# Where SyncE waits for the output: inside the block, or behind its closing barrier

## The chip, the cores and the metric

The kernel runs on one core of one Trainium2 chip. A core has five engines with a queue of instructions each: TensorE (PE in the profile, with PEld for its weight loads), VectorE (DVE), ScalarE (ACT), GpSimd (POOL) and SyncE (SP). [...] Transfers are issued by SyncE and ScalarE and run on 16 DMA engines; when one lands, its semaphore has been raised by 16 in all.

The metric is the device time of one execution in microseconds (us). The time of the kernel before is the median of three runs.

## What is computed

One decode step of a transformer layer for two sequences, B = 2, with one new token each, D = 640. In short:

```python
W = min(4096, max(256, Sk // 4))                  # 2048 of the 8192 cached keys
q = layernorm(x) @ wq                             # 32 heads of 192
p = softmax(q . k_cache[:, :, -W:] * 192 ** -0.5)
h = x + (p . v_cache[:, :, -W:]) @ wo
h2 = h + (gelu(layernorm(h) @ w_gate) * (layernorm(h) @ w_up)) @ w_down
```

All inputs are bfloat16. Only the last 2048 positions of the two caches are read, but every head has its own keys and values, so 122 MB come from memory for an output of 2 x 640 numbers (2.5 KB).

## The kernel before

The kernel records every operation first and emits it afterwards. `_Prog` keeps a list of operations per engine, works out from the tiles that each reads and writes which semaphores it must wait for (`resolve`), and `emit` writes one engine's list in the order of recording. `emit_loop` does the same for TensorE, with a loop over four groups of heads.

Loads are all issued by SyncE (line 347) into one ring of SBUF with six slots: 16 loads of keys and 16 of values, 3072 KB each, the weights of the attention, and at the end those of the feed-forward part, `w_down` in four pieces last. A load waits on SyncE until the slot that it takes has been read. Keys are transposed by TensorE (line 555) and copied out by ScalarE and VectorE (lines 564 and 567); scores, softmax and the weighted values follow a group behind.

The end of the program is what matters here. The last matmuls take the four pieces of `w_down` (line 850), VectorE copies the result to the tile `yrow` (line 856), and ScalarE issues the store of the output (line 857), whose semaphore is called `dout`. Nothing reads the output on the chip.

The emitted lists stand in a block (from line 867). A block gives each engine its own stretch of code, and ends in a barrier of all five engines, which is written when the block is closed. In that barrier ScalarE, TensorE, VectorE and SyncE each drain their pipeline, raise a common semaphore by one and wait for a release; GpSimd waits until the four have come, and releases them. In the kernel before, the block is closed together with the other contexts, when the function ends; the profile puts the barrier's instructions down to line 241. In SyncE's list one wait is written by hand behind the loads, for `dout` to reach 16. In the built program that wait is carried by SyncE's branch to the end of the block, so it stands ahead of SyncE's part of the barrier.

Of the kernel before, what the change touches and what calls it, by code (L numbers as in the profile page):

```python
# [227 lines left out]
def bass_sequential_preLN__sliding_block_cached__geglu_ffn__decode_kernel(  # L228
# [12 lines left out]
    with ExitStack() as ctx:  # L241
# [84 lines left out]
        P = _Prog()  # L326
# [535 lines left out]
        sems = {}  # L862
        for e, c in (("pe", 0), ("act", 0), ("dve", 0), ("dve", 1), ("pool", 0)):
            sems[e, c] = ctx.enter_context(nc.semaphore(f"s_{e}{c}"))
        for d in P.dma_count:
            sems["d", d] = ctx.enter_context(nc.semaphore(f"s_{d}"))
        block = ctx.enter_context(nc.Block())

        @block.gpsimd
        def _(e):  # L870
            P.emit("pool", e, sems)

        @block.sync
        def _(e):
            P.emit("sp", e, sems)
            e.wait_ge(sems["d", "dout"], 16)

        @block.vector
        def _(e):
            P.emit("dve", e, sems)  # L880

        @block.scalar
        def _(e):
            P.emit("act", e, sems)

        @block.tensor
        def _(e):
            P.emit_loop(e, sems, 4, ["a0", (0, None, ["oc"]), "a1", (0, 3, ["op"]), "a2", "b0", "b1", "b2", "c0", "c1", "c2",
                                     (None, 3, ["d0", "d1", "d2"])])


# [26 lines left out]
```

## Time and profile before

| what | value |
|---|---|
| median of three runs | 294.08 us (293.97, 294.08, 294.17) |
| span of the profiled execution, first to last instruction | 292.4 us |
| around the span (median less span) | 1.7 us |
| TensorE matmul, busy | 196.2 us, 67% |
| VectorE, busy | 128.2 us, 44% |
| ScalarE, busy | 96.3 us, 33% |
| read from memory | 122.29 MB, 418 GB/s over the span |
| issue of the output's store | starts at 290.26 us, takes 0.64 us |
| last end of the barrier's instructions | 292.4 us |

The profile is of one execution; times in its views count from the first instruction of the span. The profile gives that execution's span and no device time of its own, so the 1.7 us is the difference between the profiled execution's span and the median of other executions. "Busy" leaves out waits, branches, semaphore instructions and the issuing of transfers, which the sequencer of an engine does; in views, these have a q behind the engine's name (SPq, ACTq). A page of a profile gives the chain of waits that ended last, the groups of instructions with their idle time, and the transfers; finer views list the waits of one engine, the instructions of one line of the source, and the instructions in order of time. The trace behind them also holds every change of a semaphore, with its time, and every packet of a transfer.

### The profile page before, as it was taken

How to read it: one execution, taken by the hardware profiler on the slowest of the kernel's cores; microseconds unless marked ns; L12 is line 12 of the kernel's file. 1: busy time of each engine (PE TensorE's matmuls, PEld its weight loads, DVE VectorE, ACT ScalarE, POOL GpSimd, SP SyncE). 2: the span in 40 equal slices, each digit the busy share in tenths (PEclk: the TensorE clock that was granted, in tenths of full speed). 3: DMA queues.
4: the chain of work that ended last, by engine and by line, in shares of the span. 5: the costliest groups of instructions: out<-in, count | busy, mean ns of one | idle time of the engine just before them, and what ended most of it. 6: DMA issues, size and time to landing. Idle time of an engine off the chain costs nothing.

```text
span 292.4 us, 5066 instructions
## 1 busy us (share of the span) xinstructions
PE 196.2 (67%) x2141; PEld 151.6 (52%) x2141; DVE 128.2 (44%) x311; ACT 96.3 (33%) x120; POOL 8.6 (3%) x36
## 2 busy tenths in 40 slices
PE   2450769848677298849493597659596959585584
PEld 1440436728475285628281575456566657563242
DVE  5950075713447045525264155425265535352231
ACT  2150116623442143616161154325342525341000
POOL 4000020000000000000000000000000000000000
PEclk9996679995979579998899599969797968897755
DMA  7997999999999999999999999999999999999993
GB/s 269 430 531 338 433 447 436 430 433 430 423 408 448 430 434 428 430 430 430 430 402 450 434 430 430 430 430 434 430 430 430 430 430 434 430 430 405 425 416 148
DMA packets 6362, 122.44 MB, mean 419 GB/s; under 512 B 718, under 2 KB 848, under 8 KB 1360
## 3 DMA queue, kind: packets, MB, share of 16 engines
q1 hardware_dynamic: 6336, 122.29, 97.9%
q8 instruction: 7, 0.11, 0.2%
q14 instruction: 3, 0.02, 0.0%
q10 hardware_dynamic: 16, 0.01, 0.0%
HBM read 122.29 MB, written 0.00 MB: 418 GB/s over the span
## 4 chain that ended last, share of the span: by engine, by line
DMA 76%; PE 20%; SPq 2%; DVE 1%; issue 0%
DMA ring<-in_A_k_cache_dram 57%; PE tps L555 15%; DMA ring<-in_A_wq_dram 10%; DMA ring<-in_B_w_down_dram 10%; PE tps L576 2%; SPq L347 2%; PE ops L657 1%; PE m L708 1%; PE m L690 1%; DVE ktr L567 0%; DVE ering L408 0%; PE m L850 0%; PE m L641 0%; PE m L671 0%; DVE yrow L856 0%
## 5 line engine op out<-in xcount | busy, mean ns | idle before, releaser
L555 PE MATMUL tps<-identf,ring 128*128 128x128 f32 x768 | 114.4, 317 | 45.4 <-DMA ring<-in_A_k_cache_dram 44.1
L555 PEld LDWEIGHTS tps<-identf,ring 128*128 128x128 f32 x768 | 105.5, 166 | 48.4 <-DMA ring<-in_A_k_cache_dram 45.4
L564 ACT ACTIVATE ktr<-tps 128x1024 bf16<-128x1024 bf16 x80 | 79.4, 1023 | 84.0 <-PE tps L555 84.0
L567 DVE COPY ktr<-tps 128x1024 bf16<-128x1024 bf16 x112 | 74.0, 687 | 71.3 <-PE tps L555 70.4
L632 ACT ACTIVATE eexp<-sm,nm 128x512 bf16<-128x512 f32 x16 | 11.5, 721 | 64.1 <-DVE nm L630 64.1
L657 PE MATMUL ops<-ring,ering 128*32 128x384 bf16 x512 | 24.7, 337 | 4.8 <-DMA ring<-in_A_v_cache_dram 4.7
L613 PE MATMUL sps<-ktr,rq 128*16 128x512 bf16 x384 | 25.8, 403 | 1.1 <-POOL rq L408 1.1
L621 DVE CUSTOM_DVE_ANT_1 sm<-sps,mska 128x512 f32<-128x512 f32 x16 | 11.1, 692 | 34.9 <-PE sps L613 34.9
L657 PEld LDWEIGHTS ops<-ring,ering 128*32 128x32 bf16 x512 | 12.7, 98 | 13.3 <-DMA ring<-in_A_v_cache_dram 6.2
L613 PEld LDWEIGHTS sps<-ktr,rq 128*16 128x16 bf16 x384 | 9.5, 90 | 11.9 <-issue 2.1
L628 PEld LDWEIGHTS m<-mrhs,pm 128*128 128x128 bf16 x16 | 1.5, 96 | 22.8 <-DVE mrhs L404 22.8
L576 PE MATMUL tps<-ring,xnT 128*32 128x384 bf16 x80 | 5.7, 472 | 10.9 <-DMA ring<-in_A_wq_dram 10.9
L628 PE MATMUL m<-mrhs,pm 128*128 128x16 bf16 x16 | 2.9, 183 | 14.7 <-DVE mrhs L404 14.7
L408 POOL TENSOR_TENSOR rq<-qs,mask 128x96 bf16<-128x96 bf16 x16 | 5.6, 359 | 195.4 <-PE sps L613 161.3
L576 PEld LDWEIGHTS tps<-ring,xnT 128*32 128x32 bf16 x80 | 3.1, 134 | 13.4 <-issue 11.1
L599 DVE CAST qs<-ops 128x384 bf16<-128x384 f32 x1 | 0.6, 558 | 17.7 <-PE ops L594 17.7
L408 DVE TENSOR_TENSOR ering<-m,mask 128x256 bf16<-128x256 f32 x16 | 6.7, 419 | 3.2 <-PE m L641 3.2
L708 PE MATMUL m<-ring,ot 128*2 128x320 bf16 x96 | 4.7, 340 | 2.4 <-DMA ring<-in_A_wo_dram 2.4
L583 ACT ACTIVATE qrow<-tps 128x768 bf16<-128x768 f32 x1 | 0.8, 812 | 15.6 <-PE tps L576 15.6
L788 ACT ACTIVATE lnv<-tps,eps_t 98x1 f32<-98x1 f32 x1 | 0.3, 262 | 17.3 <-PE tps L786 17.3
L641 PE MATMUL m<-sel,eexp 128*128 128x64 bf16 x64 | 5.0, 206 | 1.2 <-ACT eexp L632 1.2
L641 PEld LDWEIGHTS m<-sel,eexp 128*128 128x128 bf16 x64 | 4.7, 111 | 1.7 <-DVE nm L630 1.3
(124 smaller groups left out, 88.8 us busy)
## 6 DMA issues: line engine op xcount, KB each, us to landing
ring<-in_A_k_cache_dram SPq DMA_DIRECT2D x16, 3072.0 KB, 31.2
ring<-in_A_v_cache_dram SPq DMA_DIRECT2D x16, 3072.0 KB, 27.3
ring<-in_A_wq_dram SPq DMA_DIRECT2D x1, 7680.0 KB, 28.3
ring<-in_A_wo_dram SPq DMA_DIRECT2D x4, 1920.0 KB, 21.5
ring<-in_B_w_gate_dram SPq DMA_DIRECT2D x1, 1920.0 KB, 31.5
ring<-in_B_w_up_dram SPq DMA_DIRECT2D x1, 1536.0 KB, 24.8
ring<-in_B_w_down_dram SPq DMA_DIRECT2D x1, 960.0 KB, 27.2
ring<-in_B_w_down_dram SPq DMA_DIRECT2D x1, 480.0 KB, 27.9
```

What stands on the lines that cost most here:

```text
L347: P.op("sp", lambda e, v=v, src=src: e.dma_start(v, src), W=toks + [("sem", sem)], dma=sem)
L408: return lambda e: e.tensor_tensor(out=out, in0=a, in1=b, op=op)
L555: ins = e.transpose(tps[bi][:, 128 * u:128 * (u + 1)], kv[:, off:off + 128], identf[:, :])
L564: act(lambda e, dst=dst, bv=bv: e.activation(out=dst, in_=bv, func=ACT.Copy), W=[("kt", n)], X=[("t", bi)])
L567: dve(lambda e, dst=dst, bv=bv: e.tensor_copy(dst, bv), W=[("kt", n)], X=[("t", bi)], cls=0)
L576: ins = e.matmul(tps[0][32 * r:32 * (r + 1), 0:384], lhsT=xnT[:, c, 32 * J:32 * (J + 1)], rhs=wq[:, c, 1536 * J + 384 * r:1536 * J + 384 * ...
L613: ins = e.matmul(sps[32 * ch:32 * ch + 16, :], lhsT=rq[:, g % 4, k, :], rhs=ktr[:, k // 2, 1024 * ch + k % 2:1024 * (ch + 1):2], start=(k ...
L621: dve(lambda e: e.tensor_tensor_reduce(out=sm[:, :].rearrange("p (u x) -> p u x", u=4), in0=sps[:, :].rearrange("p (u x) -> p u x", u=4), ...
L632: act(lambda e: e.activation(out=eexp[:, :], in_=sm[:, :], func=ACT.Exp, bias=nm[:, 0:1], scale=1.0, accum_out=zr[:, g % 4:g % 4 + 1]), R= ...
L641: ins = e.matmul(o, lhsT=eexp[:, 128 * u:128 * (u + 1)], rhs=sel64[:, :], start=True, stop=True)
L657: ins = e.matmul(ops_[32 * r:32 * (r + 1), 0:384], lhsT=ering[:, g % 4, t, :], rhs=vv[:, 384 * t:384 * (t + 1)], start=(g % 4 == 0 and t < 4),
L708: ins = e.matmul(m1[32 * r:32 * r + 2, 192:512], lhsT=ot[:, kk, :], rhs=wo[:, kk - k0, 320 * h:320 * (h + 1)], start=(kk == 1 or J < 2 and ...
```

## The change

The block is closed by a `with` statement of its own, and SyncE's wait for `dout` is written behind it, outside the block. So SyncE's branch to the end of the block waits for nothing, the barrier of the five engines is built as before (the profile will have it under line 867), and one more instruction stands behind it on SyncE alone: a wait until `dout` is 16 (line 890). The order and the waits of all other instructions of the five engines are the same. Only the indentation of the rest of the block changes.

```diff
-        block = ctx.enter_context(nc.Block())
+        with nc.Block() as block:
...
-        @block.sync
-        def _(e):
-            P.emit("sp", e, sems)
-            e.wait_ge(sems["d", "dout"], 16)
+            @block.sync
+            def _(e):
+                P.emit("sp", e, sems)
...
+        nc.sync.wait_ge(sems["d", "dout"], 16)
```

More of the change, by code (lines that the diff above doesn't have):

```diff
@@ L866, in bass_sequential_preLN__sliding_block_cached__geglu_ffn__decode_kernel, with _ @@
             sems["d", d] = ctx.enter_context(nc.semaphore(f"s_{d}"))
-        block = ctx.enter_context(nc.Block())
-        @block.gpsimd
-        def _(e):
-            P.emit("pool", e, sems)
-        @block.sync
-        def _(e):
-            P.emit("sp", e, sems)
-            e.wait_ge(sems["d", "dout"], 16)
[L878 to L889, printed above, removed]
+        with nc.Block() as block:
+            @block.gpsimd
+            def _(e):
+                P.emit("pool", e, sems)
+            @block.sync
+            def _(e):
+                P.emit("sp", e, sems)
+            @block.vector
+            def _(e):
+                P.emit("dve", e, sems)
+            @block.scalar
+            def _(e):
+                P.emit("act", e, sems)
+            @block.tensor
+            def _(e):
+                P.emit_loop(e, sems, 4, ["a0", (0, None, ["oc"]), "a1", (0, 3, ["op"]), "a2", "b0", "b1", "b2", "c0", "c1", "c2",
+                                         (None, 3, ["d0", "d1", "d2"])])
+        nc.sync.wait_ge(sems["d", "dout"], 16)
 _INS = ['A_x', 'A_k_cache', 'A_v_cache', 'A_wq', 'A_wo', 'B_x', 'B_w_gate', 'B_w_up', 'B_w_down']
```

## The prediction

> **What bounds the kernel now**
>
> I read the page first, for the share of each engine and of the transfers; then the chain of waits to its last step; then the waits of SyncE's queue, since the edit moves one of them; then the instructions of the line on which the closing barrier is put down (L241). The page:
>
> ```profile
> span 292.4 us, 5066 instructions
> ...
> HBM read 122.29 MB, written 0.00 MB: 418 GB/s over the span
> ...
> DMA 76%; PE 20%; SPq 2%; DVE 1%; issue 0%
> ```
>
> The kernel is bound by reading 122 MB; its chain is 76% transfers. Nothing there is touched. The end of the chain:
>
> ```profile
> 260.85 28.24 DMA ring<-in_B_w_down_dram
> 289.09 0.04 issue
> 289.14 0.74 PE m L850 x12
> 289.88 0.02 issue
> 289.91 0.32 DVE yrow L856
> ```
>
> The last weights land at 289.09, twelve matmuls and one copy follow, and the chain of working instructions stops at 290.23. The span has 2.1 us more. The timeline's only line behind that copy, and SyncE's longest late wait:
>
> ```profile
> 290.26 0.64 ACTq L857 DMA_DIRECT2D out_dram<-yrow  x1
> ```
>
> ```profile
> SPq L241 <- DMA out_dram<-yrow: 26.4, 1, 26.4
> ```
>
> SyncE issued its last load by 265.6 and then sat 26.4 us on the output's semaphore. Nothing but the closing barrier stands behind that wait on its queue, but four other engines stand in the barrier. The barrier's own instructions (count, duration in ns min/median/max, first and last start):
>
> ```profile
> engine op xcount: duration ns min/median/max, first and last start us, forms
> L241 POOLq EVENT_SEMAPHORE  x2: 17/17/17, 292.2 to 292.3; - x2
> L241 POOLq DRAIN  x1: 457/457/457, 204.2 to 204.2; - x1
> L241 PEldq DRAIN  x1: 372/372/372, 289.5 to 289.5; - x1
> L241 DVEq DRAIN  x1: 364/364/364, 289.9 to 289.9; - x1
> L241 ACTq DRAIN  x1: 485/485/485, 290.9 to 290.9; - x1
> L241 SPq COMPARE_BRANCH  x1: 33/33/33, 292.0 to 292.0; - x1
> L241 SPq DRAIN  x1: 13/13/13, 292.2 to 292.2; - x1
> L241 SPq EVENT_SEMAPHORE  x1: 17/17/17, 292.3 to 292.3; - x1
> ...
> L241 PEldq EVENT_SEMAPHORE  x1: 51/51/51, 292.3 to 292.3; - x1
> ```
>
> The reader is to see the order: POOL, PE, DVE and ACT are drained long before SyncE. The trace's records have the same in ns, with the semaphore events, which no view prints. ACT's drain starts at 290.948 and its arrival is counted at 291.441. The output's last increment comes at 291.977; SyncE's branch, which carries the wait, runs at 291.994, its drain at 292.154, its arrival is counted at 292.168. POOL sees all four at 292.192 and releases them at 292.295; SyncE's last instruction ends at 292.329, PE's at 292.375, and that is the span's end.
>
> **What lies around the span.** The median of 294.08 is 1.7 us over the span. The records go on behind the span: semaphore 2, which the kernel does not own, is counted up five times at 292.614, .649, .859, .904 and .928, four times more at 293.029, .068, .104 and .151; then each engine clears a block of semaphores until 293.715, and the nine counts come again from 293.939 to 294.299. The same nine stand ahead of the kernel, from -0.372 to 0.001. There the engines start their first instruction in the order SyncE 0.000, DVE 0.129, POOL 0.135, ACT 0.146, PE 0.321, which fits nine counts passed from PE over ACT, POOL and DVE to SyncE and back, each engine counting only after the one ahead. By that reading the third of the five, POOL, was late at 292.859: it followed ACT by 210 ns where it followed by 38 ns ahead of the kernel and again in the second round.
>
> **The change part by part**
>
> (1) *The wait leaves SyncE's last branch.* No work, no transfer and no instruction before the barrier changes on any engine. SyncE's branch and drain (33 and 13 ns, 0.17 us between the wake-up and the arrival, 291.994 to 292.168) run after the last load is issued, at about 266 us, and are hidden by the 26.4 us wait that ends the kernel anyway. If that cover were gone they would cost those 0.17 us again.
>
> (2) *The barrier closes on ACT.* The last arrival becomes ACT's, 291.441 instead of 292.168: 0.727 us earlier. POOL's collecting and release follow as before: release at 292.295 - 0.727 = 291.57, SyncE free at 291.60, PE at 291.65. ACT's drain of 485 ns is now what the barrier waits for; it is hidden by the output's landing, with 291.977 - 291.60 = 0.38 us to spare.
>
> (3) *SyncE gets one instruction behind the barrier,* a wait on the output's semaphore. It is satisfied at 291.977 as before, starts at 291.994 (as the branch did) and takes the 17 ns of SyncE's other semaphore wait: ends at 292.011. Queued behind it on SyncE is only the closing round of semaphore 2, in which all engines take part. So the span ends at 292.01 instead of 292.375, 0.36 us earlier, and SyncE leaves 292.329 - 292.011 = 0.318 us earlier.
>
> (4) *The closing round.* POOL leaves 0.727 earlier, so its late count moves from 292.859 to 292.132, if its lateness goes with its leaving. DVE follows by 45 ns (292.177) and SyncE can count at 292.201 at the earliest. When SyncE itself is ready the trace of before does not show, since it waited there for POOL. Bounds: from its end at 292.329 to its count at 292.928 is 0.60 us, so after the change it counts no later than 292.61 (gain 0.32); no earlier than 292.201 (gain 0.727). The nearest row is PE's, the first in the round, which waits for nobody: from its end at 292.375 to its count at 292.614, 0.239 us. Ahead of the kernel SyncE needs about the same, 0.231 us from its count to its first instruction. I take 0.24: the fifth count at 292.25 instead of 292.928, **0.68 us earlier**. Everything behind it (clearing, second round) follows the fifth count and keeps its length.
>
> [...] The trace has 0.78 us from the last leaving to the ninth count, and 0.21 of it is one engine's lateness.
>
> Sum: 294.08 - 0.68 = 293.40, with the offset of 1.7 us reckoned as a stretch in which the closing rounds lie.
>
> **The rivals**
>
> *A, the forecast:* SyncE and POOL both reach the round early. Gain 0.59 to 0.727, time 293.35 to 293.49. For it: PE's 0.239 and the entry's 0.231. Against it: the fifth count's place within the metric is only inferred from 294.08 exceeding the span by 1.7.
>
> *B, only SyncE's own shift counts.* Either SyncE is as slow as its bound (0.60 us from its end to its count), or the third engine in the round is SyncE, or the time stops before the round. Then the gain is 0.32 to 0.36 us: 293.72 to 293.76. For it: 0.21 us of lateness would suit an engine that left last, and SyncE had its wait and branch just before. Against it: PE left 46 ns after SyncE and counted first.
>
> *C, the change buys nothing.* POOL's lateness is tied to something that does not move, such as the output's landing at 291.977; its count stays at 292.859 and the time at 294.08. Nothing in the records names such a thing.
>
> *D, slower: a code fetch comes onto the path.* The four engines run into the closing code 0.7 us early and SyncE stops at a wait one instruction further down its code. If the block with the closing code then has to be fetched while SyncE stands there, that fetch is paid behind 292.011. Instruction packets in the trace take 0.31 to 0.53 us (8192 B) or 1.06 us (16384 B, at 286.955); the gain of 0.68 is the point from which it decides. One large fetch gives 294.08 - 0.68 + 1.06 = 294.46; two in a row 295.5. For it: one 8192 B packet at 293.522 took 531 ns, in the closing stretch. Against it: that packet came behind the round, and only one instruction is added. [...]
>
> **How the numbers follow.** Chances: A 0.52, B 0.37, C 0.06, D 0.05. The time is A's, 293.40. The range runs from A's cap of 293.35, with the 0.1 us by which the three runs differ from their median, to B's 293.76 with the same: 293.25 to 293.90; C and D, 0.11, are left out. A change of 0.2%, 0.59 us, is about what a measurement of this kernel can tell from none. Faster by more is A alone, 0.52; slower by more is D with more than one large fetch, 0.03; the rest is within, 0.45.
>
> **What the changed profile would show.** Step 1: SyncE's branch and drain of the closing line start near 266 us instead of 292. Step 2: the two POOL semaphore instructions start at about 291.5, the four releases at about 291.6, 0.15 us behind ACT's counted arrival. Step 3: one semaphore wait on SyncE's own line (L890) of 17 ns, last in the span, at 292.0, with a span of 292.0 and a wait of some 0.4 us on the output instead of 26.4. Step 4: the fifth count of semaphore 2 at about 0.24 us behind SyncE's last end, 292.25, and the third count near 292.13. The prediction is wrong if the third count keeps its distance from SyncE's end (B), if it stays at 292.86 (C), or if an instruction packet stands between SyncE's end and its count (D). It is wrong in another way if the output lands later than 1.06 us behind the end of ACT's issue (290.908 to 291.977), since every step from 3 on hangs on that.

## The result, and the profile after

The changed kernel takes 293.29 us (median of 9 runs, 293.20 to 293.38), the kernel before 293.99 us (9 runs, 293.95 to 294.17). The ratio is 0.9975 with a 95% interval of 0.9966 to 0.9983: 0.70 us by the medians, 0.5 to 1.0 us by the interval. By the median that is 0.25% faster; the interval lies wholly on the faster side, but its slow end, 0.17%, is under the 0.2% that the prediction took as the least that can be told. Run again later (11 runs against 33), the two kernels gave 293.32 against 294.08, ratio 0.9977 (0.9968 to 0.9986).

The page of the changed kernel, its span and the shares of the chain of waits:

```profile
span 291.9 us, 5066 instructions
...
DMA 76%; PE 20%; SPq 2%; DVE 1%; issue 0%
```

The reading of memory bounds it as before. The chain's end (start, duration in us):

```profile
260.82 28.19 DMA ring<-in_B_w_down_dram
289.01 0.04 issue
289.05 0.74 PE m L850 x12
289.79 0.02 issue
289.81 0.33 DVE yrow L856
```

The copy of the result begins 0.09 us earlier than in the profile of before (289.81 against 289.91). That is what two executions differ by ahead of the change; so the times behind it are compared below from the start of this copy. SyncE's queue, what it waited for (us in total, times, longest):

```profile
SPq L867 <- PEq L867: 25.9, 1, 25.9
...
SPq L890 <- DMA out_dram<-yrow: 0.4, 1, 0.4
```

The 26.4 us that SyncE waited for the output are now 25.9 us in the barrier (which GpSimd releases; the view names TensorE, which changes the same semaphore) and 0.4 us behind it. The instructions of the barrier's line, and of the wait's line behind it (duration in ns, first and last start in us):

```profile
L867 POOLq EVENT_SEMAPHORE  x2: 17/17/17, 291.4 to 291.5; - x2
...
L867 SPq DRAIN  x1: 129/129/129, 265.5 to 265.5; - x1
...
L867 ACTq DRAIN  x1: 485/485/485, 290.9 to 290.9; - x1
L867 SPq EVENT_SEMAPHORE  x1: 17/17/17, 291.5 to 291.5; - x1
...
```

```profile
L890 SPq EVENT_SEMAPHORE  x1: 17/17/17, 291.9 to 291.9; - x1
```

SyncE drains at 265.5, ScalarE is the last to reach the barrier (its arrival is counted at 291.350), all are released at 291.5 (291.478), and the wait for the output is the last instruction of the span.

What the views do not print are the nine counts of semaphore 2 behind the span, which the prediction was about. Read from the traces, in us from the start of the copy to `yrow` ("last leaving" is the end of the last instruction of the span, and the "second nine" are the counts that come again behind a stretch in which the semaphores from 7 to 255 change, in five blocks: 292.227 to 292.895 in the changed kernel. That this is a clearing, one block to an engine, is the author's reading; the traces show the changes and their times). The rows behind the second are the kernels of the experiments below:

| kernel | output landed | last leaving | 1st count | 3rd | 4th | 5th | 9th | last of the second nine |
|---|---|---|---|---|---|---|---|---|
| before | 2.070 | 2.468 | 2.707 | 2.952 | 2.997 | 3.021 | 3.244 | 4.392 |
| changed | 2.069 | 2.103 | 1.981 | 2.227 | 2.272 | 2.295 | 2.516 | 3.662 |
| GpSimd waits | 2.064 | 2.105 | 1.979 | 2.647 | 2.691 | 2.714 | 2.935 | 4.081 |
| TensorE waits | 2.067 | 2.146 | 2.342 | 2.415 | 2.459 | 2.482 | 2.702 | 3.850 |
| SyncE, 2 more instructions | 2.070 | 2.235 | 1.979 | 2.225 | 2.271 | 2.352 | 2.516 | 3.662 |
| SyncE, 8 more instructions | 2.067 | 2.595 | 1.980 | 2.226 | 2.271 | 2.712 | 2.876 | 4.020 |
| store from SyncE | 2.065 | 2.098 | 1.974 | 2.220 | 2.265 | 2.288 | 2.510 | 3.655 |
| no block | 2.066 | 2.100 | 0.139 | 1.643 | 1.687 | 2.227 | 2.389 | 3.610 |
| waits on both sides | 2.066 | 2.495 | 2.703 | 2.949 | 2.995 | 3.018 | 3.239 | 4.384 |
| changed, run again | 2.069 | 2.103 | 1.980 | 2.226 | 2.271 | 2.295 | 2.516 | 3.661 |

From before to changed the output lands at the same place, the last engine leaves 0.365 us earlier, and the last count of the second nine comes 0.730 us earlier. The device time fell by 0.70 us, so it goes with the counts and not with the span.

Each row above is one execution. The runs behind them give the time and the span of the same execution, so the part of the time that lies outside the span can be compared without a start to count from (means of 9 to 11 executions, 66 for before; the spans are on record to 0.1 us):

| kernel | trace: last leaving to last count of the second nine | runs: time less span |
|---|---|---|
| before | 1.92 | 1.82 |
| changed | 1.56 | 1.45 |
| GpSimd waits | 1.98 | 1.87 |
| TensorE waits | 1.70 | 1.60 |
| SyncE, 2 more instructions | 1.43 | 1.33 |
| SyncE, 8 more instructions | 1.43 | 1.33 |
| store from SyncE | 1.56 | 1.45 |
| no block | 1.51 | 1.54 |
| waits on both sides | 1.89 | 1.79 |
| changed, run again | 1.56 | 1.46 |

In nine of the ten rows the two columns differ by 0.10 us, while each of them moves by up to 0.5 us from row to row: the time moves with the last count. The kernel without a block is the exception, by 0.13 us.

### The profile page after: what moved, and what is told of

The parts are those of the page before. It is cut to its first block, busy times and chain, and to the rows that moved or that the text cites. A ratio compares the mean times of both kernels' runs of the same rounds, so it can differ in the third digit from the quotient of the medians.

```text
span 291.9 us, 5066 instructions
## 1 busy us (share of the span) xinstructions
PE 197.7 (68%) x2141; PEld 153.8 (53%) x2141; DVE 128.4 (44%) x311; ACT 96.2 (33%) x120; POOL 8.6 (3%) x36
## 4 chain that ended last, share of the span: by engine, by line
DMA 76%; PE 20%; SPq 2%; DVE 1%; issue 0%
DMA ring<-in_A_k_cache_dram 57%; PE tps L555 16%; DMA ring<-in_A_wq_dram 10%; DMA ring<-in_B_w_down_dram 10%; SPq L347 2%; PE tps L576 2%; PE ops L657 1%; PE m L708 1%; PE m L690 1%; DVE ering L408 0%; PE m L641 0%; PE m L850 0%; DVE ktr L567 0%; PE m L671 0%; DVE yrow L856 0%
## 5 line engine op out<-in xcount | busy, mean ns | idle before, releaser
L555 PE MATMUL tps<-identf,ring 128*128 128x128 f32 x768 | 116.7, 322 | 46.8 <-DMA ring<-in_A_k_cache_dram 45.7
L555 PEld LDWEIGHTS tps<-identf,ring 128*128 128x128 f32 x768 | 107.9, 169 | 49.8 <-DMA ring<-in_A_k_cache_dram 47.1
L613 PE MATMUL sps<-ktr,rq 128*16 128x512 bf16 x384 | 24.6, 388 | 1.1 <-POOL rq L408 1.1
L576 PE MATMUL tps<-ring,xnT 128*32 128x384 bf16 x80 | 5.0, 422 | 9.0 <-DMA ring<-in_A_wq_dram 9.0
L708 PE MATMUL m<-ring,ot 128*2 128x320 bf16 x96 | 5.5, 381 | 1.6 <-DMA ring<-in_A_wo_dram 1.6
L408 DVE TENSOR_TENSOR orow<-m,wm 128x1536 bf16<-128x1536 f32 x3 | 5.3, 1751 | 0.0
```

The source lines that it names most:

```text
L408: return lambda e: e.tensor_tensor(out=out, in0=a, in1=b, op=op)
L555: ins = e.transpose(tps[bi][:, 128 * u:128 * (u + 1)], kv[:, off:off + 128], identf[:, :])
L576: ins = e.matmul(tps[0][32 * r:32 * (r + 1), 0:384], lhsT=xnT[:, c, 32 * J:32 * (J + 1)], rhs=wq[:, c, 1536 * J + 384 * r:1536 * J + 384 * ...
L613: ins = e.matmul(sps[32 * ch:32 * ch + 16, :], lhsT=rq[:, g % 4, k, :], rhs=ktr[:, k // 2, 1024 * ch + k % 2:1024 * (ch + 1):2], start=(k ...
L708: ins = e.matmul(m1[32 * r:32 * r + 2, 192:512], lhsT=ot[:, kk, :], rhs=wo[:, kk - k0, 320 * h:320 * (h + 1)], start=(kk == 1 or J < 2 and ...
```

## The experiments

All were run beside the kernel before, on the same chip; each has 11 runs against 33 of before, and the ratios are to these. The two kernels of the first section and the two of the second ran on one chip (before: 294.05 us), the other four, with the changed kernel once more, on another (before: 294.08 us).

### The wait behind the barrier on another engine

By the order that the prediction read, GpSimd is third in the closing round and TensorE first. If the time follows the round, it should rise; if it follows the span, it should not.

```diff
-        nc.sync.wait_ge(sems["d", "dout"], 16)
+        nc.gpsimd.wait_ge(sems["d", "dout"], 16)
```

> The changed kernel, but the wait for the output behind the barrier stands on GpSimd instead of SyncE. Theory (the closing round of semaphore 2 is what the time follows, and GpSimd, third in it, counts 0.57 us after its last instruction): GpSimd's last instruction ends with the output's landing, at about 291.92 on the scale of the changed kernel's profile instead of 291.47; third count near 292.49, fifth near 292.56 instead of 292.11. Time 0.45 us over the changed kernel: 293.74, some 0.27 us under the kernel before. Rival 1 (the time follows the last instruction of the span, whichever engine has it): span 291.9 as in the changed kernel, time 293.29. Rival 2 (SyncE's leaving is what counts): SyncE now leaves at 291.51, 0.41 us earlier than in the changed kernel, time about 292.9.

293.70 us, ratio 0.9990 (0.9981 to 0.9999). The span and the last instruction, from the view of the cores and the instructions of the wait's line:

```profile
core 0: 291.6 us, clock 0.841
```

```profile
L890 POOLq EVENT_SEMAPHORE  x1: 17/17/17, 291.6 to 291.6; - x1
```

The span of this profile is the shortest of all eight experiments (its copy began 0.29 us earlier than the changed kernel's), and yet this execution took 293.49 us, 0.13 us more than the changed kernel's profiled one, and the median lies 0.41 us over the changed kernel's. From the copy, the last engine leaves at 2.105 against 2.103, but the third count moves from 2.227 to 2.647, and all behind it by 0.42. GpSimd's count comes 0.542 us after its end; in the kernels before and changed it was 0.572. The rival of the span falls, and so does that of SyncE's leaving, which expected the time to fall.

```diff
-        nc.sync.wait_ge(sems["d", "dout"], 16)
+        nc.tensor.wait_ge(sems["d", "dout"], 16)
```

> The changed kernel, but the wait for the output behind the barrier stands on TensorE, which is first in the round. Theory: TensorE's wait takes 51 ns, ends at 291.95 and is followed by its count 0.24 us later, 292.19; the others are ready and follow with 35, 38, 45 and 24 ns: fifth count 292.33, 0.22 us over the changed kernel, time 293.51. Rival 1 (last instruction of the span): 0.03 us over the changed kernel, 293.32. Rival 2 (SyncE's leaving): about 292.9.

293.48 us, ratio 0.9982 (0.9973 to 0.9991). By the time alone this can't be told from the changed kernel, as the intervals overlap; the trace tells it. TensorE's count comes 0.196 us after its end, the others follow one another at 34, 39, 44 and 23 ns, as they did ahead of the kernel before (35, 38, 45 and 23), and the ninth count is 0.186 us behind that of the changed kernel; the medians differ by 0.19 us. The reading of the order, TensorE first and GpSimd third, is borne out by these two runs: each moved the count that it should. The places of ScalarE and VectorE, second and fourth, were not tried.

### How much slack SyncE has

```diff
         nc.sync.wait_ge(sems["d", "dout"], 16)
+        for _ in range(4):
+            nc.sync.wait_ge(sems["d", "dout"], 16)
```

> The changed kernel with four more waits for the output behind the first on SyncE; in the built program they are two more instructions. They wait for nothing, so they delay SyncE's leaving by about 2 x 0.08 us (GpSimd's two semaphore instructions at the barrier start 0.078 us apart). Theory (GpSimd's late count limits the round, SyncE has a slack of up to 0.19 us): 0 to 0.16 us over the changed kernel, 293.29 to 293.45, and the distance from SyncE's end to the fifth count shrinks. Rivals 1 and 2 (span, or SyncE's leaving): the whole 0.16 us, 293.45, the distance stays 0.19.

293.31 us, ratio 0.9977 (0.9968 to 0.9986): no change from the changed kernel, although SyncE leaves 0.13 us later. The waits on SyncE's line are three instructions; the two added ones carry two waits each:

```profile
L892 SPq EVENT_SEMAPHORE  x3: 17/28/28, 291.8 to 291.9; - x3
```

The fifth count follows SyncE's end by 0.117 us, where it was 0.192 in the changed kernel, and comes 0.057 us later; but the sixth count (VectorE's on the way back, by the order that the prediction read) comes 0.044 us behind the fifth instead of 0.101, and the ninth count is where it was, at 2.516.

With sixteen more:

> The changed kernel with sixteen more waits for the output behind the first on SyncE; in the built program they are eight more instructions, about 8 x 0.08 = 0.62 us. Theory: SyncE is now the last to count in the round; the time rises by 0.62 less SyncE's slack of up to 0.19 us, to 293.72 to 293.91, and the distance from SyncE's end to the fifth count is its own transit, which the kernel before hid (0.19 us or less). Rivals 1 and 2: the whole 0.62 us, 293.91, distance 0.19.

293.63 us, ratio 0.9988 (0.9979 to 0.9997). The waits on SyncE's line:

```profile
L892 SPq EVENT_SEMAPHORE  x9: 17/28/28, 291.8 to 292.2; - x9
```

Nine instructions, starting 0.060 us apart instead of the 0.078 that was assumed, so SyncE leaves 0.49 us later (2.595 against 2.103). The distance to the fifth count is 0.117 us again: that is SyncE's own way into the round, and the round now stands still for SyncE. The ninth count is 0.36 us later, the median by 0.34; with the shorter step of 0.060 us the time came out below the 293.72 to 293.91 that was expected. So from SyncE's leaving to the ninth count the changed kernel hides 0.13 us: 0.075 behind GpSimd's count and 0.058 between the fifth count and the sixth, which is VectorE's by the order that the prediction read.

### The old wait put back beside the new one

```diff
                 P.emit("sp", e, sems)
+                e.wait_ge(sems["d", "dout"], 16)
```

> The changed kernel with the old wait put back inside the block as well: SyncE waits for the output ahead of the barrier and once more behind it. Theory (it is the barrier's wait on SyncE that counts, not the closing of the block by a with statement): the time of the kernel before, 294.05; the extra instruction delays SyncE by about 0.06 us, which GpSimd's late count hides. If the earlier closing of the block were what counts: 293.3.

294.07 us, ratio 1.0001 (0.9992 to 1.0010): the whole gain is gone. SyncE's branch carries the wait again, from the instructions of the barrier's line:

```profile
L867 SPq COMPARE_BRANCH  x1: 33/33/33, 291.8 to 291.8; - x1
L867 SPq DRAIN  x1: 13/13/13, 291.9 to 291.9; - x1
```

Every count of the first nine is within 5 ns of the kernel before, and the last of the second nine within 8 ns, with one instruction more on SyncE (2.495 against 2.468 for the last leaving). Closing the block by a `with` statement changes nothing that can be measured here; the wait ahead of the barrier is the cost.

### Two attempts to go further

The store could be issued by SyncE, so that the barrier need not stand behind ScalarE's issue and drain.

```diff
-        P.op("act", lambda e: e.dma_start(out[:, 0, :].rearrange("b (r n) -> r b n", r=4), yrow[0:113:16, :]), R=["y"], W=["out"],
+        P.op("sp", lambda e: e.dma_start(out[:, 0, :].rearrange("b (r n) -> r b n", r=4), yrow[0:113:16, :]), R=["y"], W=["out"],
```

> The changed kernel with the output's store issued by SyncE instead of ScalarE (SyncE waits for the copy, issues, joins the barrier, then waits for the landing). ScalarE then drains early and the barrier no longer stands behind its 0.64 us issue and 0.485 us drain, but behind SyncE's issue and its short drain (0.13 us in the changed kernel's profile). Theory: the barrier closes some 0.3 us earlier, GpSimd's count moves with it, and SyncE, which needs 0.117 us from its end to its count (as the runs with more waits showed), becomes the last: fifth count near 292.04 instead of 292.11 on the scale of the changed kernel's profile, the ninth some 0.13 us earlier because VectorE's way back is then hidden. Time 293.16, 0.13 us under the changed kernel. Rival 1 (the span): the span is the same as the landing is, 293.29. Rival 3 (GpSimd's count does not follow its leaving): 293.29.

293.37 us, ratio 0.9977 (0.9968 to 0.9986), against 293.32 of the changed kernel on that chip: no gain. The drains of the barrier's line:

```profile
L867 ACTq DRAIN  x1: 611/611/611, 285.4 to 285.4; - x1
...
L867 SPq DRAIN  x1: 423/423/423, 290.8 to 290.8; - x1
```

SyncE's drain, 129 ns in the changed kernel, takes 423 ns right behind the issue of a store, nearly as much as ScalarE's 485; and SyncE's issue took 690 ns, where ScalarE's took 644. The barrier closed 6 ns earlier than with ScalarE, and the expectation fell with the drain. The 129 ns that it had taken are no sign of a queue at rest: that drain, too, stood right behind an issue, of the last load, which had ended 0.06 us before. That issue had taken 4.16 us, the store's 0.69; why the one drain is short and the other long stays open.

Or the block is left out, so that no engine but SyncE is late:

```diff
-        with nc.Block() as block:
...
+        P.emit("pool", nc.gpsimd, sems)
+        P.emit("sp", nc.sync, sems)
+        P.emit("dve", nc.vector, sems)
+        P.emit("act", nc.scalar, sems)
+        P.emit_loop(nc.tensor, sems, 4, ["a0", (0, None, ["oc"]), "a1", (0, 3, ["op"]), "a2", "b0", "b1", "b2", "c0", "c1", "c2",
+                                         (None, 3, ["d0", "d1", "d2"])])
```

> The changed kernel without any block: the same lists of instructions, written straight behind the opening of the program, so that there is no closing barrier at all and no branches or drains of it; SyncE still waits for the output at its end. Theory: GpSimd leaves at about 204 us, TensorE, VectorE and ScalarE by 290.9; SyncE alone is late. It ends at 291.92 and counts 0.117 us later at 292.04; ninth count near 292.20 instead of 292.33. Time 293.16, as with the store on SyncE. Rival 1 (the span): 293.29. A rival on the barrier's worth (the barrier itself costs what it takes from ScalarE's arrival to the last release, 0.2 us, beyond what the round hides): 293.1 or less.

293.34 us, ratio 0.9977 (0.9968 to 0.9986): no gain over the changed kernel's 293.32. The round itself did what was expected: GpSimd is long there (its count follows ScalarE's by 0.039 us), the fifth count comes 0.127 us after SyncE's end, and the ninth at 2.389 instead of 2.516. But the second nine end only 0.052 us earlier. The block of semaphore changes that the author puts down to VectorE, by the order of the round (from semaphore 156 on in the changed kernel), starts 0.14 us behind the sixth count in the changed kernel (292.211 to 292.354) and 0.64 us behind it here (291.937 to 292.576), and the fourth count of the second nine stands 0.125 us behind the third, where the changed kernel has 0.044. Why is open: no instruction packet lies in that stretch of the trace. Nor does the time follow the counts fully: less the span it is 0.08 us longer than the changed kernel's (1.54 against 1.46), where the counts end 0.05 us earlier. These 0.13 us are open too.

The changed kernel was run unedited beside these, to compare them with:

> The changed kernel itself, as the measure for the three others on the same chip. All theories: 293.29, 0.70 us under the kernel before.

293.32 us, ratio 0.9977 (0.9968 to 0.9986).

A kernel without any wait for the output was not tried, since its output might not have landed when the program ends.

## Why the prediction was right

The forecast was 293.40 us with a gain of 0.68; measured are 293.29 and 0.70. Of the 0.11 us between the two times 0.09 is the kernel before: 294.08 us in the three runs that the forecast started from, 293.99 us in nine. That the gains agree to 0.02 us is in part luck: the counts moved by 0.73, and the medians gave 0.70 and, run again, 0.76. Step by step:

- **Step 1, the wait leaves the branch.** Held. SyncE's drain ran at 265.5 under the long wait. It took 129 ns there instead of 13, which costs nothing.
- **Step 2, the barrier closes on ScalarE.** Held. The release came 2.388 us after the copy's start before and 1.663 after, 0.725 earlier where 0.727 was said, and ScalarE's drain kept its 485 ns.
- **Step 3, one instruction behind the barrier.** Held. It starts 17 ns behind the last landing, takes 17 ns, and the span shrank by 0.365 us from the copy on, where 0.36 was said. The raw spans differ by more, 292.4 to 291.9, as the copy began 0.09 us earlier.
- **Step 4, the closing round.** The mechanism held: GpSimd's count moved with its leaving (0.572 us from end to count, before and after). Mis-sized was the one term that the trace of before could not show, SyncE's way from its end to its count. It was taken from TensorE's as 0.24; it is 0.117, as the two runs with more waits showed. So SyncE was ready 0.05 us before the fourth count (VectorE's by the order read), and the gain went to the bound that the step named as the earliest possible, 0.727: the fifth count moved by 0.726 from the copy on. What follows the fifth count kept its length here (1.371 and 1.367 us to the last count), as forecast; it is not fixed, since it became 0.06 us shorter where SyncE came later.
- **The offset around the span.** That the 1.7 us hold the closing rounds was inferred from their size, with a span and a time of different executions; of the same executions it is 1.82 us. The inference held: where the experiments moved the last count of the second nine, the time less the span moved with it to 0.01 us, but for the kernel without a block.

Of the rivals, B (only SyncE's own shift, 0.32 to 0.36 us) falls in each of its forms: SyncE's count came 0.192 us behind its end in the changed kernel and not 0.60, the third count moved with GpSimd's wait, and with that wait the time rose although the last leaving stayed and SyncE left earlier. C falls with the third count, which moved by 0.725. D falls too: the only late instruction packet stands at 292.70, behind the fifth count at 292.11, as it had stood behind it before. What such a packet costs an engine that has to wait for it was not shown. What lies behind the last leaving is no fixed stretch in these runs: from there to the ninth count are 0.78 us before, 0.41 us in the changed kernel and 0.83 us with the wait on GpSimd. It went with who left last and how far the others were.

## What to carry to other kernels

In this kernel the wait for the output ahead of the closing barrier held up five engines and put the whole barrier, 0.40 us from the landing to the last leaving, behind a landing that one engine can watch. Behind the barrier, on the engine with the shortest way out of the three tried (0.117 us from its end to its count, against 0.196 on TensorE and 0.542 on GpSimd), it cost nothing here: the round waited for GpSimd, and SyncE had 0.13 us to spare. What is left ahead of GpSimd's count is the barrier behind ScalarE's issue (644 ns) and drain (485 ns). Which engine waits matters as much as where: the same wait gave 293.3 us on SyncE, 293.5 on TensorE and 293.7 on GpSimd, with the same last leaving to 0.04 us. And the span is not the time (from the copy on the span shrank by 0.365 us, the time by 0.70): where a change touches the last microseconds, the semaphore events behind the last instruction belong to the reading.

## What the runs showed of the hardware that was not expected

- The engines differ in their way from the kernel's last instruction to their first closing count: SyncE 0.117 us (0.127 without a block), TensorE 0.196 to 0.239, GpSimd 0.542 to 0.572. What GpSimd does in that time the trace does not show. Without a block ScalarE, whose last instruction is then the store's issue, counted 0.60 us behind the end of that issue (1.002 to 1.604), 0.08 us behind the end of its drain in the changed kernel (1.528).
- A drain on SyncE took 13 ns behind a long wait, 129 ns right behind the issue of its last load and 423 ns right behind a store's issue; on ScalarE 485 ns behind the same issue.
- An instruction with two semaphore waits that are already met cost SyncE 0.060 us from start to start. Two of them changed nothing (293.31 us), as the round waited for GpSimd; eight moved the ninth count by 0.36 us.
